# A guard's norms computed on TensorE instead of VectorE, and four lent buffers, in a planned attention kernel

## The chip, the cores and the metric

The kernel runs on one core of a Trainium2 chip. A core has engines with instruction streams of their own: TensorE (PE, with its weight loads PEld) multiplies matrices, VectorE (DVE) and ScalarE (ACT) work element by element, GpSimd (POOL) has little to do here, and SyncE (SP) issues transfers (DMAs). They tell each other of finished work by semaphores. Data lies in SBUF (128 partitions); TensorE's results arrive in PSUM, eight banks of 128 x 512 fp32. The metric is the time of one execution in microseconds (us), as the median of several runs.

## The reference

```python
def _A_ref(x, wqkv, wo):                      # x: 1 x 2048 x 640, 32 heads of 20
    qkv = (x @ wqkv).reshape(B, S, 3, H, Dh).transpose(2, 0, 3, 1, 4)
    q, k, v = qkv[0], qkv[1], qkv[2]
    scores = jnp.einsum("bhqd,bhkd->bhqk", q, k) * Dh ** -0.5
    p = softmax(scores)
    o = jnp.einsum("bhqk,bhkd->bhqd", p, v)
    return o.transpose(0, 2, 1, 3).reshape(B, S, D) @ wo

def _B_ref(x, w1, b1, w2):                    # 640 -> 1536 -> 640
    h = x @ w1 + b1
    sp = log1p(exp(-abs(h))) + where(h > 0, h, 0)
    return (h * tanh(sp)) @ w2                # mish

g = sigmoid((x * gate_w).sum(-1, keepdims=True))
out = g * _A_ref(x, wqkv, wo) + (1 - g) * _B_ref(x, w1, b1, w2)
```

Branch A is full attention, branch B a dense layer with the mish activation, and a gate per row mixes the two. All is bf16 with fp32 accumulation. The work that counts is the exponential: 32 heads x 2048 x 2048 scores.

## The kernel before, in words

**Units and slots.** The scores are computed in units of 128 keys x 512 queries of one head; there are 2048. Three units make a slot, 683 in all. For each slot TensorE writes the scores into three PSUM banks (`score_mms`, L1058), ScalarE turns all of them into bf16 exponentials by one instruction (`emit_e`, L1080, buffer `ETS`), and TensorE multiplies these with the values into one accumulating bank (`pv`, L1183), four heads side by side. Two sets of three banks take turns, so the scores of slot s + 2 may be written only when the exponentials of slot s have been read; meanwhile ScalarE works on slot s + 1. The last bank (`FB`) serves all other products.

**Units on VectorE.** In some slots the third unit isn't left to ScalarE, whose instruction is then two units wide (128 x 1024). VectorE computes its exponential in four instructions: `emit_x` reads the scores out of PSUM (L1097), two steps of a polynomial run in `EM` or `ER` (L1113), and a last one writes the result (L1115). The unit lives in a home: a buffer of 128 x 512 of four bytes. There are five (`UNITS`), used in turn: two in `XE` and three in a work area that lies in `W2R` and later in `REG`. A home is busy until the value product has read it. `choose` decides slot by slot whether a unit goes to VectorE, by VectorE's backlog and by when the unit's group ends (`CHAIN` is part of that sum). Before, 207 units go there.

**Groups.** 64 units of a group (one block of 512 queries, four heads) accumulate in one bank. VectorE copies it out (`OUNG`, L1261); three small transfers on SyncE's queue and VectorE's reciprocal and product (L1229) normalise it.

**Other tasks.** Between the slots TensorE does the rest in pieces of a few matmuls, as tasks with due slots: key, query and value projections (`kq_task` L539, `k_task` L591, `v_task` L685, `v_pair_task` L712), the first layer of branch B (`h_task`, L848, in half-chunks `hc` of 256 rows, with the bias added on VectorE, L858, into `HB`), its second layer (`b_task`, L909, whose output goes to `XS` for the first two row blocks and later to parts of `XB`), and the output projection (`p_task`, L933 and L939).

**The planner.** The kernel is built by a plan in Python: `Plan.add` puts an instruction on an engine's list and keeps an estimated clock per engine, from costs per instruction (`EXP`, `WIDE`, `PASS`). The loop over slots emits a slot's exponential, then the scores of the slot after next, value products and portions of due tasks, as far as the estimated time allows. VectorE's pieces wait in lists and are placed into estimated gaps (`work`). `fill_up` repeats scores or issues a spare product (L1442) where the estimated share of streaming columns of TensorE in a window falls below `STREAM` or `SPUN`. So the order on each engine is fixed when the kernel is built, and any change of a cost, a limit or a task moves all later instructions.

**The guard.** The softmax subtracts no maximum. A guard bounds the scores by the norms of the rows of queries' and keys' weights and of x: it computes the largest column sums of squares. Before, `squares` squares Wq, Wk and x on VectorE (40 instructions, L754) into `HB`, in eight tasks `sq_task`; TensorE sums each over the partitions with a column of ones (L770), and VectorE takes the maximum of the one row that results (L779). `flag_ops` combines the eight maxima (L1357 to L1363) into `FLAG`, which every engine loads (L1372); if it is set, a second program does everything again with maxima. It isn't set for these inputs. `h_task` waits until all eight squares have been read, since they lie in `HB`.

The functions that the change touches follow, with the line numbers of the profile.

Of the kernel before, what the change touches and what calls it, by code (L numbers as in the profile page):

```python
# [51 lines left out]
STREAM = 0.49  # L52
# [11 lines left out]
CHAIN = 3.3  # L64
# [32 lines left out]
UNITS = 5  # L97
ULPS = 128 / math.log(2)
# [118 lines left out]
def bass_gated_mix__softmax_full_mha__dense_activation_mish__prompt_kernel(  # L217
# [51 lines left out]
    MXS = sb("MXS", [1, 8], FP32)  # L269
    MXR = sb("MXR", [1, 4], FP32)  # L270
# [6 lines left out]
    def xt(c):  # L277
        return XB[:, c, :].rearrange("p (f t) -> p f t", t=CW)
# [29 lines left out]
    def ei(home):  # L308

        area, b = home  # L310
        return XE[:, b - 3, :] if b >= 3 else AREAS[area][1][:, b * CW:(b + 1) * CW]
# [22 lines left out]
    def attention(pl, fast):  # L334
# [122 lines left out]
        if fast:  # L457
# [284 lines left out]
            sq_ops, sq_read, sq_max = {}, {}, []  # L742

            def sq_src(n):
                return (WQ, WK)[n // 2][:, :, n % 2 * HALF:(n % 2 + 1) * HALF] if n < 4 else xt(n - 4)

            def squares(n):

                src = sq_src(n)
                after = [w_load[k] for k in (("wq", "wq0"), ("wk", "wk0"))[n // 2]] if n < 4 else xt_load[n - 4]  # L750

                def square(f):
                    dst = HB[:, n % 2, :, :].rearrange("p f t -> p (f t)")[:, f * CW:f * CW + src.shape[2]]
                    op = pl.add("dve", lambda e: e.tensor_tensor(dst, src[:, f, :], src[:, f, :], ALU.mult),  # L754
                                [*after, sq_read.get(n - 2)], cost=0.5)
                    sq_ops.setdefault(n, []).append(op)
                    if n < 4:
                        (wq_read, wkv_read)[n // 2].append(op)
                    else:
                        x_read[n - 4].append(op)  # L760

                for f in range(NFT):
                    bg.append((0.5, lambda f=f: square(f), lambda: max(after, key=lambda o: o.t1)))

            def sq_task(n, due):

                w = HALF if n < 4 else CW

                def mm(f):
                    return lambda e, bank: e.matmul(  # L770
                        PS[0:1, bank, 0:w], V_all[:, 0, 0, 0:1],
                        HB[:, n % 2, :, :].rearrange("p f t -> p (f t)")[:, f * CW:f * CW + w],
                        start=(f == 0), stop=(f == NFT - 1))

                def finish(bank, last):
                    sq_read[n] = last
                    if n + 2 < 8:
                        squares(n + 2)
                    ev = dve(lambda e: e.tensor_reduce(MXS[0:1, n:n + 1], PS[0:1, bank, 0:w], AX.X, ALU.max),  # L779
                             [last, *sq_max[-1:]], 0.69)  # L780
                    sq_max.append(ev)
                    if n == 7:
                        bg.append((0.5, lambda: flag_ops(ev), None))
                    return ev

                return Task([mm(f) for f in range(NFT)], w * COL, finish, due,
                            lambda: [*sq_ops[n], m_one] if len(sq_ops.get(n, ())) == NFT else None)
# [4 lines left out]
            def load_w1(n):  # L792

                k = n % 6
                if n < 2:
                    deps = []
                elif n in (FIRST, FIRST + 1):
                    assert len(sq_ops) >= 4
                    deps = list(wkv_read)
                else:  # L800
                    deps = [w1_last[n - 2]]
# [11 lines left out]
            def load_wo():  # L813
                assert len(sq_ops) >= 4
# [25 lines left out]
            def h_task(hc, k, due):  # L840
# [11 lines left out]
                def finish(bank, last):  # L852
                    x_read[c].append(last)
                    w1_last[n1] = last
                    if n1 + 2 < FIRST or FIRST <= n1 < 6 * NHC - 2:
# [4 lines left out]
                        [last, *b1f, *sq_read.values(), *b_read.get(hc - 2, [])], WIDE)  # L860
# [827 lines left out]
```

## Time and profile before

| | |
|---|---|
| median of 3 runs | 874.08 us (873.82 to 874.53) |
| the profiled execution | 874.34 us |
| its span, first to last instruction | 871.9 us |
| busy: ScalarE, VectorE, TensorE | 855.7, 831.2, 753.4 us |
| granted TensorE clock, mean | 0.998 |
| exponentials on ScalarE | 475 of three units, 208 of two |

Engine times are unions of the records. Records of ScalarE and TensorE overlap their neighbours, since an instruction is recorded from its entry into the engine's pipe to its end; a mean duration is longer than the pace at which instructions follow each other. In groups, the columns are the line, engine, operation, output and inputs with shapes, and the count; then busy time, the mean of one in ns, and the idle time ahead of it with what ended it. In the timeline the first two columns are the start and the length in us of a row, which may merge several instructions (xN).

### The profile page before, as it was taken

To read this page: it belongs to the slowest core of one execution; us is meant where nothing else is said; L and a number is where in the kernel's file an instruction comes from. 1 tells how busy PE (TensorE), PEld (TensorE's weight loads), DVE (VectorE), ACT (ScalarE), POOL (GpSimd) and SP (SyncE) were. 2 spreads that over 40 slices of the span, in tenths; PEclk is the share of its full clock that TensorE was granted. 3 is DMA by queue.
4 is the path that set the end of the run, shared out by engine and by line. 5 is a ranking of instruction groups with operands and counts; after the bars stand their busy time and mean duration, and the time that the engine had idled before them with its cause. 6 is when DMAs were issued, how large, how long until landed. Compare 5 with 4: busy or idle time off the path is not lost.

```text
span 871.9 us, 15314 instructions
## 1 busy us (share of the span) xinstructions
PE 753.4 (86%) x6244; PEld 258.2 (30%) x6293; DVE 831.2 (95%) x1441; ACT 855.7 (98%) x714; POOL 15.7 (2%) x29
## 2 busy tenths in 40 slices
PE   7888888889888888898888888898888888998895
PEld 3222332223322232232222333232333333332232
DVE  4899999999999999999999999999999999999995
ACT  6999999999999999999999999999999999999996
POOL 2000000000000000000000000000000000000000
PEclk9999999999999999999999999999999999999999
DMA  9112100012222111311111211111212112010001
GB/s 211 34 50 67 56 27 13 3 43 63 58 71 70 42 41 44 104 32 39 44 48 47 71 43 47 32 32 56 63 38 66 53 47 68 16 33 14 14 14 35
DMA packets 69870, 42.44 MB, mean 49 GB/s; under 512 B 20472, under 2 KB 65776, under 8 KB 69744
## 3 DMA queue, kind: packets, MB, share of 16 engines
q1 hardware_dynamic: 67424, 40.89, 16.5%
q8 instruction: 52, 0.85, 0.4%
q10 hardware_dynamic: 2256, 0.47, 0.3%
q0 software_dynamic: 112, 0.01, 0.2%
q14 instruction: 26, 0.21, 0.1%
HBM read 33.97 MB, written 5.23 MB: 45 GB/s over the span
## 4 chain that ended last, share of the span: by engine, by line
ACT 95%; PE 2%; DMA 1%; DVE 1%; SPq 0%; issue 0%; ACTq 0%
ACT ETS L1080 92%; ACT REG L880 2%; DMA BCT<-SUMS 1%; DMA OTN<-in_A_x_dram 1%; ACT W2R L880 1%; PE PS L1058 1%; PE PS L1183 0%; PE PS L539 0%; PE PS L909 0%; PE PS L659 0%; DVE HB L939 0%; DVE XE L1097 0%; PE PS L650 0%; SPq L583 0%; PE PS L1442 0%
## 5 line engine op out<-in xcount | busy, mean ns | idle before, releaser
L1080 ACT ACTIVATE ETS<-PS 128x1536 bf16<-128x1536 f32 (+1 forms) x683 | 836.6, 1501 | 0.8 <-PE PS L1058 0.7
L1058 PE MATMUL PS<-QT,KT 32*128 32x512 bf16 (+1 forms) x2191 | 275.9, 377 | 99.4 <-ACT ETS L1080 85.5
L1183 PE MATMUL PS<-ETS,V_all 128*21 128x512 bf16 (+1 forms) x1897 | 210.6, 379 | 1.0 <-ACT ETS L1080 0.5
L1058 PEld LDWEIGHTS PS<-QT,KT 32*128 32x128 bf16 x2191 | 68.3, 91 | 316.1 <-ACT ETS L1080 294.6
L1183 PEld LDWEIGHTS PS<-ETS,V_all 128*21 128x21 bf16 x1897 | 48.5, 89 | 95.9 <-issue 89.4
L909 PE MATMUL PS<-W2R,HB 128*128 128x320 bf16 x384 | 73.0, 302 | 0.4 <-DVE XB L916 0.2
L1113 DVE SCALAR_TENSOR_TENSOR EM<-EM 128x512 f32<-128x512 f32 x104 | 70.7, 679 | 0.1
L1113 DVE SCALAR_TENSOR_TENSOR ER<-ER 128x512 f32<-128x512 f32 x103 | 70.1, 681 | 0.0
L1097 DVE TENSOR_SCALAR XE<-PS 128x512 f32<-128x512 f32 x82 | 56.1, 684 | 3.2 <-PE PS L1058 1.9
L848 PE MATMUL PS<-XB,REG 128*128 128x256 bf16 x360 | 55.7, 275 | 1.2 <-DVE HB L858 0.6
L1097 DVE TENSOR_SCALAR REG<-PS 128x512 f32<-128x512 f32 x76 | 52.1, 686 | 4.0 <-PE PS L1058 2.6
L539 PE MATMUL PS<-XB,WOQ 128*128 128x512 bf16 x135 | 41.3, 383 | 2.8 <-issue 2.1
L909 PEld LDWEIGHTS PS<-W2R,HB 128*128 128x128 bf16 x384 | 28.7, 97 | 36.0 <-issue 23.3
L1097 DVE TENSOR_SCALAR W2R<-PS 128x512 f32<-128x512 f32 x49 | 33.4, 682 | 3.4 <-PE PS L1058 2.9
L848 PEld LDWEIGHTS PS<-XB,REG 128*128 128x128 bf16 x360 | 27.8, 97 | 26.8 <-issue 24.8
L858 DVE TENSOR_TENSOR HB<-PS,B1F 128x512 bf16<-128x512 f32 x48 | 32.7, 682 | 0.4 <-PE PS L848 0.3
L898 DVE SCALAR_TENSOR_TENSOR U<-U 128x512 f32<-128x512 f32 x48 | 32.7, 681 | 0.0
L899 DVE SCALAR_TENSOR_TENSOR U<-U,HB 128x512 f32<-128x512 f32 x48 | 32.5, 677 | 0.0
L1442 PE MATMUL PS<-KT 128*128 128x512 bf16 x100 | 30.2, 383 | 1.6 <-issue 1.3
L1113 DVE SCALAR_TENSOR_TENSOR EM<-XE 128x512 f32<-128x512 uint16 x41 | 28.0, 683 | 0.3
L1113 DVE SCALAR_TENSOR_TENSOR ER<-XE 128x512 f32<-128x512 uint16 x41 | 27.9, 681 | 0.2
L1115 DVE SCALAR_TENSOR_TENSOR XE<-ER,XE 128x512 int32<-128x512 f32 x41 | 27.9, 681 | 0.0
(115 smaller groups left out, 815.7 us busy)
## 6 DMA issues: line engine op xcount, KB each, us to landing
REG<-in_B_w_dram SPq DMA_DIRECT2D x36, 320.0 KB, 3.2
BCT<-SUMS SPq DMA_DIRECT2D x31, 256.0 KB
W2R<-in_B_w_dram SPq DMA_DIRECT2D x12, 320.0 KB, 3.3
KT<-KS SPq DMA_DIRECT2D x28, 128.0 KB
KS<-OTN SPq DMA_DIRECT2D x16, 128.0 KB, 1.7
W2R<-in_B_w_dram SPq DMA_DIRECT2D x1, 1920.0 KB, 7.9
out_dram<-OUTT SPq DMA_DIRECT2D x24, 80.0 KB, 1.6
REG<-in_A_wqkv_dram SPq DMA_DIRECT2D x2, 700.0 KB, 8.6
```

Source lines behind the costliest of these rows:

```text
L539: return lambda e, bank: e.matmul(PS[:, bank, :], pads[:, b, f, :], xt(c)[:, f, :], start=(f == 0), stop=(f == NFT - 1))
L848: return lambda e, bank: e.matmul(PS[:, bank, i * HW:(i + 1) * HW], w1b(n1)[:, f, i * P:(i + 1) * P], xt(c)[:, f, cols], start=(f == 0), s ...
L858: ev = dve(lambda e: e.tensor_tensor(hb, PS[:, bank, :].rearrange("p (i t) -> p i t", i=2), bias, ALU.add), [last, *b1f, *sq_read.values() ...
L898: piece(WIDE, lambda e: e.scalar_tensor_tensor(U2[:, :], U2[:, :], EVEN[0], U2[:, :], ALU.add, ALU.mult))
L899: piece(WIDE, lambda e, to=to: e.scalar_tensor_tensor(U2[:, :], U2[:, :], EVEN[1], to, ALU.add, ALU.mult))
L909: return lambda e, bank: e.matmul(PS[:, bank, 0:HALF], HB[:, hc % 2, f, t * P:(t + 1) * P], W2[:, f, half * HALF:(half + 1) * HALF], start ...
L1058: op = pl.add("pe", lambda e, i=i, g=real(g), tile=tile, j=j, cols=cols, c=c, of_q=of_q: e.matmul(scores(s)[:, i, cols], KT[32 * j:32 * j ...
L1080: e_op[s] = pl.add("act", lambda e: e.activation(ETS[:, s % NETS, 0:n, :], scores(s)[:, 0:n, :], AF.Exp, scale=SCALE, bias=LIFT if fast el ...
L1097: ev_op[s] = dve(lambda e: e.tensor_scalar(y, scores(s)[:, 2, :], SCALE * ULPS, BIAS, ALU.mult, ALU.add), [s_op[s], ei_free[b], *(wkv_read ...
L1113: piece(WIDE, lambda e, v=m if i else f, i=i: e.scalar_tensor_tensor(m, v, STEPS[i], v, ALU.add, ALU.mult), lambda i=i: () if i else [lane ...
L1183: lasts[n] = pl.add("pe", lambda e, tile=tile, h=real(g) * HG + j, j=j, src=src[:, cols], of_q=of_q, count=count: e.matmul(PS[32 * j:32 * ...
L1442: pl.add("pe", lambda e: e.matmul(PS[:, bank, :], k[:, 0:P], k, start=True, stop=True), [free], cost=PASS, kind="S")
```

## The change

Three things change together.

- The guard's column sums of squares are the diagonals of products of a block of 128 columns with itself. `gram_task` has TensorE multiply each block of Wq, Wk and x by itself, five row tiles accumulated: four blocks to a bank, seven tasks (130 products of 128 x 128). VectorE takes one maximum per bank over all entries (an entry off the diagonal can't exceed the largest on it). The result is a maximum per partition, so `flag_ops` first combines columns on 128 partitions, then a transfer on SyncE's queue puts 128 x 3 numbers into one row (`U2`), and `flag_end` takes their maximum and goes on as before.
- Since nothing is squared into `HB`, its second half (until half-chunk 1 writes it) and `XS` (until the first row blocks of branch B do) are lent as four more homes (`LENT`). `home` now takes the free home that has been free longest. `back` ends the lending, and the first writers wait for the value products that read them.
- `CHAIN` goes from 3.3 to 3.9 and `STREAM` from 0.49 to 0.48.

With these limits the plan puts 211 units on VectorE.

```diff
 EXP = 1.335
-STREAM = 0.49
+STREAM = 0.48
 SPUN = 0.6
...
 RISK = {"pe": 0.1, "act": 0.3, "dve": 0.5, "pool": 1.2, "sp": 0.6}
-CHAIN = 3.3
+CHAIN = 3.9
 AHEAD = 14
...
 UNITS = 5
+LENT = (("h", 0), ("h", 1), ("h", 2), ("x", 0))
 ULPS = 128 / math.log(2)
...
     GW = sb("GW", [P, NFT], BF16)
-    MXS = sb("MXS", [1, 8], FP32)
-    MXR = sb("MXR", [1, 4], FP32)
+    MXS = sb("MXS", [P, 8], FP32)
+    MXR = sb("MXR", [P, 4], FP32)
     FLAG = sb("FLAG", [1, 1], I32)
...
         area, b = home
+        if area == "h":
+            return HB[:, 1, 4 * b:4 * b + 4, :].rearrange("p f t -> p (f t)").bitcast(I32)
+        if area == "x":
+            return XS[:, 0:2 * CW].bitcast(I32)
         return XE[:, b - 3, :] if b >= 3 else AREAS[area][1][:, b * CW:(b + 1) * CW]
...
-            sq_ops, sq_read, sq_max = {}, {}, []
-
-            def sq_src(n):
-                return (WQ, WK)[n // 2][:, :, n % 2 * HALF:(n % 2 + 1) * HALF] if n < 4 else xt(n - 4)
-
-            def squares(n):
-
-                src = sq_src(n)
-                after = [w_load[k] for k in (("wq", "wq0"), ("wk", "wk0"))[n // 2]] if n < 4 else xt_load[n - 4]
-
-                def square(f):
-                    dst = HB[:, n % 2, :, :].rearrange("p f t -> p (f t)")[:, f * CW:f * CW + src.shape[2]]
-                    op = pl.add("dve", lambda e: e.tensor_tensor(dst, src[:, f, :], src[:, f, :], ALU.mult),
-                                [*after, sq_read.get(n - 2)], cost=0.5)
-                    sq_ops.setdefault(n, []).append(op)
-                    if n < 4:
-                        (wq_read, wkv_read)[n // 2].append(op)
+            grams = {}
+            guarded = []
+
+            def gram_task(n, due):
+
+                both = (w_load["wq"], w_load["wq0"], w_load["wk"], w_load["wk0"])
+                needs = both[0:2] if n == 0 else both[2:4] if n == 1 else both if n == 2 else xt_load[n - 3]
+                blocks = [(WQ, WK)[n] for _ in range(4)] if n < 2 else [WQ, WK] if n == 2 else [xt(n - 3)] * 4
+
+                def mm(b, f):
+                    at = 4 if n == 2 else b
+                    block = blocks[b][:, f, at * P:(at + 1) * P]
+                    return lambda e, bank: e.matmul(
+                        PS[:, bank, b * P:(b + 1) * P], block, block, start=(f == 0), stop=(f == NFT - 1))
+
+                def finish(bank, last):
+                    for reads in ([wq_read], [wkv_read], [wq_read, wkv_read])[n] if n < 3 else [x_read[n - 3]]:
+                        reads.append(last)
+                    if n == 2:
+                        to, src = MXS[:, 1:4:2], PS[:, bank, 0:2 * P].rearrange("p (a b) -> p a b", b=P)
                     else:
-                        x_read[n - 4].append(op)
-
-                for f in range(NFT):
-                    bg.append((0.5, lambda f=f: square(f), lambda: max(after, key=lambda o: o.t1)))
-
-            def sq_task(n, due):
-
-                w = HALF if n < 4 else CW
-
-                def mm(f):
-                    return lambda e, bank: e.matmul(
-                        PS[0:1, bank, 0:w], V_all[:, 0, 0, 0:1],
-                        HB[:, n % 2, :, :].rearrange("p f t -> p (f t)")[:, f * CW:f * CW + w],
-                        start=(f == 0), stop=(f == NFT - 1))
-
-                def finish(bank, last):
-                    sq_read[n] = last
-                    if n + 2 < 8:
-                        squares(n + 2)
-                    ev = dve(lambda e: e.tensor_reduce(MXS[0:1, n:n + 1], PS[0:1, bank, 0:w], AX.X, ALU.max),
-                             [last, *sq_max[-1:]], 0.69)
-                    sq_max.append(ev)
-                    if n == 7:
-                        bg.append((0.5, lambda: flag_ops(ev), None))
-                    return ev
-
-                return Task([mm(f) for f in range(NFT)], w * COL, finish, due,
-                            lambda: [*sq_ops[n], m_one] if len(sq_ops.get(n, ())) == NFT else None)
+                        to, src = MXS[:, (0, 2, 0, 4, 5, 6, 7)[n]:][:, 0:1], PS[:, bank, :]
+                    grams[n] = dve(lambda e: e.tensor_reduce(to, src, AX.X, ALU.max), [last], WIDE)
+                    if len(grams) == 7:
+                        bg.append((0.3, lambda: flag_ops(grams.values()), None))
+                    return grams[n]
+
+                return Task([mm(b, f) for b in range(len(blocks)) for f in range(NFT)], 0.06, finish, due,
+                            lambda: list(needs))
...
                 elif n in (FIRST, FIRST + 1):
-                    assert len(sq_ops) >= 4
+                    assert all(n in grams for n in range(3))
                     deps = list(wkv_read)
...
             def load_wo():
-                assert len(sq_ops) >= 4
+                assert all(n in grams for n in range(3))
                 wo_v = A_wo.rearrange("(g j r) c -> j r g c", g=NG, j=HG, r=DH)
...
                         hb, PS[:, bank, :].rearrange("p (i t) -> p i t", i=2), bias, ALU.add),
-                        [last, *b1f, *sq_read.values(), *b_read.get(hc - 2, [])], WIDE)
+                        [last, *b1f, *guarded, *b_read.get(hc - 2, []), *lent("h", hc == 1)], WIDE)
                     if k % 2:
...
                 def ready():
-                    if len(acts) > 1 or len(sq_read) < 8 or n1 not in w1_load or (hc >= 2 and len(b_read.get(hc - 2, ())) < 4):
+                    if len(acts) > 1 or not guarded or n1 not in w1_load or (hc >= 2 and len(b_read.get(hc - 2, ())) < 4):
+                        return None
+                    if hc == 1 and not back("h"):
                         return None
...
                         OMG[:, tb:tb + 1], None, ALU.mult),
-                        [last, gate_done[0], *(x_read[(hc - 1) // 2] if hc else ())], HALVED)
+                        [last, gate_done[0], *(x_read[(hc - 1) // 2] if hc else lent("x"))], HALVED)
                     bdone[(tb, half)] = ev
...
                         return None
-                    if any((hc, k) not in h_done for k in range(6)):
+                    if any((hc, k) not in h_done for k in range(6)) or hc == 0 and not back("x"):
                         return None
...
         ei_free.update({(None, b): None for b in range(3, UNITS)})
+        ei_free.update({at: None for at in LENT})
+        given_back = set()
         area = [0]
...
+        def lent(name, here=True):
+
+            return [op for at, op in ei_free.items() if here and at[0] == name and op is not None]
+
+        def back(name):
+
+            given_back.add(name)
+            return "busy" not in lent(name)
+
         def home():
-            b = nx[0] % UNITS
-            return (None if b >= 3 else area[0], b)
+            some = [(None if b >= 3 else area[0], b) for b in range(UNITS)]
+            some += [at for at in LENT if at[0] not in given_back]
+            some = [at for at in some if ei_free[at] != "busy"]
+            return min(some, key=lambda at: ei_free[at].t1 if ei_free[at] else 0.0, default=None)
...
             ev_op[s] = dve(lambda e: e.tensor_scalar(y, scores(s)[:, 2, :], SCALE * ULPS, BIAS, ALU.mult, ALU.add), [
-                s_op[s], ei_free[b], *(wkv_read if b[0] else ())], WIDE)
+                s_op[s], ei_free[b], *(wkv_read if b[0] == 1 else ())], WIDE)
             last = [ev_op[s]]
...
             urgent, other = (sum(t[0] for todo in some for t in todo) for some in ((norm, *soon), (blend, bg)))
-            if (len(order) < SLOT or ei_free[home()] == "busy"
+            if (len(order) < SLOT or home() is None
                     or late + urgent + other >= BEHIND):
...
             assert all(t.due < last_kv.due for t in tasks[tasks.index(last_q) + 1:-1])
-            tasks.extend(sq_task(n, SQ + SQ_STEP * n) for n in range(8))
+            tasks.extend(gram_task(n, SQ + SQ_STEP * n) for n in range(7))
             tasks.extend(h_task(hc, k, H_AT + int(H_STEP * (6 * hc + k))) for hc in range(2) for k in range(6))
...
-        def flag_ops(last):
-
-
-            m = MXR[0:1, :]
+        def flag_ops(deps):
+
+            m = MXR[:, :]
+            row = U2[0:1, 0:3 * P]
             a = pl.add("dve", lambda e: e.tensor_reduce(
-                m, MXS[0:1, :].rearrange("o (a b) -> o a b", b=2), AX.X, ALU.max), [last])
+                m, MXS[:, :].rearrange("p (a b) -> p a b", b=2), AX.X, ALU.max), list(deps))
             a = pl.add("dve", lambda e: e.tensor_tensor(m[:, 2:3], m[:, 2:3], m[:, 3:4], ALU.max), [a])
+            moved = pl.add("sp", lambda e: e.dma_start(row, m[:, 0:3], allow_slow_non_contiguous=True), [a], "mx", tail=4.0)
+            bg.append((0.8, lambda: flag_end(row, moved), lambda: moved))
+
+        def flag_end(row, moved):
+
+            m = MXR[0:1, 0:3]
+            a = pl.add("dve", lambda e: e.tensor_reduce(
+                m, row.rearrange("o (p a) -> o a p", a=3), AX.X, ALU.max), [moved], cost=0.5)
+            guarded.append(a)
             for n in (2, 0, 1):
...
                 load_w2()
-            if fast and step == SQ - 18:
-                squares(0)
-                squares(1)
             if acts and safe(acts[0][0]) < pl.now["act"] and mish_free():
```

## The prediction

> **What bounds the kernel now.** I read the page first, then ScalarE's instructions by form, the chain that ended last in order of time, and the busy time of the engines (PE, its weight loads, DVE, ACT, POOL, then the clock) in the stretch of the exponentials and after it.
>
> ```profile
> span 871.9 us, 15314 instructions
> PE 753.4 (86%) x6244; PEld 258.2 (30%) x6293; DVE 831.2 (95%) x1441; ACT 855.7 (98%) x714; POOL 15.7 (2%) x29
> PEclk9999999999999999999999999999999999999999
> ACT 95%; PE 2%; DMA 1%; DVE 1%; SPq 0%; issue 0%; ACTq 0%
> ```
>
> ```profile
> L1080 ACT ACTIVATE ETS<-PS 128x1536 bf16<-128x1536 f32 x475 | 679.1, 1626 | 0.8 <-PE PS L1058 0.7
> L1080 ACT ACTIVATE ETS<-PS 128x1024 bf16<-128x1024 f32 x208 | 233.2, 1215 | 0.0
> ```
>
> ```profile
> 635.55 0.94 ACT REG L880
> 636.49 15.76 ACT ETS L1080 x13
> 652.24 0.94 ACT REG L880
> 653.18 16.18 ACT ETS L1080 x13
> ```
>
> ```profile
> 10.50:863.05 852.55, 742.63 (x6182) 253.44 (x6228) 823.08 (x1425) 852.23 (x708) 10.48 (x19) 1.00 0.16 47
> 863.05:871.90 8.85, 2.68 (x18) 1.21 (x19) 2.99 (x7) 0.53 (x1) 0.86 (x1) 0.83 0.19 56
> ```
>
> The exponentials on ScalarE are the kernel: 683 slots, 475 of them three units wide and 208 two wide (207 slots whose third unit is computed on VectorE, and the last slot, which has only two). From 10.50 to 863.05 us ScalarE is busy for 852.23 of 852.55 us, with them and 24 tanh at 0.94 us. The records overlap, so their means are no pace. The stretches of 13 exponentials are: 16.18 and 15.76 us differ by 0.42, one two-wide slot more. The pace itself, and what is lost to waits too short to show as idle, is in the timeline:
>
> ```profile
> 77.07 4.82 ACT L1080 ACTIVATE ETS<-PS 128x1536 bf16<-128x1536 f32 x4
> 78.76 0.39 PE L1058 MATMUL PS<-QT,KT 32*128 32x512 bf16 x3 [0.40 <-ACT ETS L1080]
> 79.08 0.40 PE L1183 MATMUL PS<-ETS,V_all 128*21 128x512 bf16 x4
> 79.64 0.38 PE L539 MATMUL PS<-XB,WOQ 128*128 128x512 bf16 x1 [0.16 <-DVE EM L1113]
> 79.95 0.39 PE L1058 MATMUL PS<-QT,KT 32*128 32x512 bf16 x3
> ```
>
> ```profile
> 78.40 1.22 ACT L1080 ACTIVATE ETS<-PS 128x1024 bf16<-128x1024 f32 x1
> 79.30 1.24 ACT L1080 ACTIVATE ETS<-PS 128x1024 bf16<-128x1024 f32 x1
> 80.39 1.50 ACT L1080 ACTIVATE ETS<-PS 128x1536 bf16<-128x1536 f32 x1
> ```
>
> A three-wide slot starts at 77.07 and the next at 78.40: 1.33 us. A two-wide one takes 0.90 (78.40 to 79.30). But the second two-wide in a row lasts 1.09, to 80.39: its successor's scores started only at 79.95, 1.19 after the scores before them (78.76), because TensorE had four value products and projections to do between. So 0.19 us is lost with no idle time on the page. A worse one shows as idle:
>
> ```profile
> 272.12 0.39 PE L1058 MATMUL PS<-QT,KT 32*128 32x512 bf16 x3
> 272.45 0.82 PE L539 MATMUL PS<-XB,WOQ 128*128 128x512 bf16 x3
> 273.20 0.40 PE L1183 MATMUL PS<-ETS,V_all 128*21 128x512 bf16 x4
> 273.53 0.69 PE L1058 MATMUL PS<-QT,KT 32*128 32x512 bf16 x6
> 273.96 1.45 ACT L1080 ACTIVATE ETS<-PS 128x1536 bf16<-128x1536 f32 x1 [0.20 <-PE PS L1058]
> ```
>
> Three projections and four value products lay between scores 1.41 us apart, 0.5 more than ScalarE's 0.90; of that 0.20 shows as idle time. At 1.33 and 0.90 the exponentials come to 475 x 1.33 + 208 x 0.90 = 819; 852.6 less the tanh (24 x 0.94 = 22.6) is 830. So 10 to 11 us are lost to such lateness (9.7 when I add it up start by start). Sorted by what the program orders between two scores, 6.8 of it falls on slots that follow two two-wide slots. So the bound is ScalarE, and behind two two-wide slots it is TensorE.
>
> **The change part by part.** *Units.* The order of the changed kernel has 212 two-wide slots instead of 208 and 471 three-wide. Saved on ScalarE: 4 x 0.43 = 1.7 us, all of it on the chain. By the two forms' means it is 4 x 0.41 (1626 less 1215 ns), by the stretches 4 x 0.42: 1.6 to 1.7.
>
> *Where they lie.* The planner moves everything, so lateness is counted anew in TensorE's order. I weigh the matmuls between two scores at these spacings: 0.22 us for a projection of 512 columns (0.82 less 0.38, over two), 0.14 for 320, 0.11 for 256, 0.06 for 128, 0.22 for a group of value products. Before, slots behind two two-wide ones:
>
> - over 0.7 us of work: 10 of them, 2.8 us lost (0.28 each; first at 38.91 us, last the one below);
> - 0.6 to 0.7: 19, 2.8 us lost (0.15 each; that of 80.39 is one);
> - less: 42, 1.1 us lost.
>
> ```profile
> 843.68 1.34 ACT L1080 ACTIVATE ETS<-PS 128x1024 bf16<-128x1024 f32 x1
> 844.98 1.02 ACT L1080 ACTIVATE ETS<-PS 128x1024 bf16<-128x1024 f32 x1
> ```
>
> Here 1.30 us passed instead of 0.90. In the changed order there are 18 of the first kind, 12 of the second and 34 of the third; three of the 18 (slots 9, 73, 141) have the very three projections and four value products of 273.96. At the same prices: 18 x 0.28 + 12 x 0.15 + 0.9 = 7.7, so 0.9 more than 6.8. The other slots lost 2.9; slots behind one two-wide slot with over 0.8 us of work grow from 21 to 37, at 0.04 each, so 0.6 more. Taken: 1.5 us more lateness. The ends: at 0.19 for each of the 18, 0.05 of the 12 and 0.9 it is 4.9, 1.9 less than now; at 0.40 and 0.25 it is 11.1, 4.3 more. I take the means, since they are from the same patterns, and keep the ends for the range.
>
> *VectorE.*
>
> ```profile
> L754 DVE TENSOR_TENSOR HB<-XB 128x512 bf16<-128x512 bf16 x20 | 8.1, 415 | 0.0
> L754 DVE TENSOR_TENSOR HB<-REG 128x320 bf16<-128x320 bf16 x10 | 3.1, 315 | 1.1 <-PE PS L770 1.1
> L754 DVE TENSOR_TENSOR HB<-WOQ 128x320 bf16<-128x320 bf16 x10 | 3.1, 340 | 0.0
> L779 DVE TENSOR_REDUCE MXS<-PS 1x1 f32<-1x512 f32 x4 | 2.7, 672 | 0.0
> L779 DVE TENSOR_REDUCE MXS<-PS 1x1 f32<-1x320 f32 x4 | 1.9, 476 | 0.3 <-PE PS L770 0.3
> L1097 DVE TENSOR_SCALAR XE<-PS 128x512 f32<-128x512 f32 x82 | 56.1, 684 | 3.2 <-PE PS L1058 1.9
> ```
>
> Removed: 8.1 + 3.1 + 3.1 + 2.7 + 1.9 = 18.9 us. Added: six maxima over 128x512 at 0.67 (the row is of one partition; the 128-partition read of PSUM in the last row is 0.68), a seventh over half as much at 0.4, one over 384 elements at 0.5, and four units of four instructions at 0.68 = 10.9; together 15.8. VectorE is 3 us lighter of 831. On the path: nothing, it released no late score in the cases I followed.
>
> *TensorE.*
>
> ```profile
> L770 PE MATMUL PS<-HB,V_all x40: 297/338/379, 33.7 to 206.5; 128*1 128x320 bf16 x20, 128*1 128x512 bf16 x20
> 6.39 1.01 PEld L650 LDWEIGHTS PS<-OTN 128*128 128x128 bf16 x18 [0.91 <-DMA OTN<-in_A_x_dram]
> 6.39 1.18 PE L650 MATMUL PS<-OTN 128*128 128x128 bf16 x18 [0.73 <-DMA OTN<-in_A_x_dram]
> ```
>
> Forty products leave, at 0.14 and 0.22: 7.2 us. The 130 of 128x128, each with its own weights, come: at 1.18/18 = 0.066 they are 8.5 us, in 16 portions of 3 to 13 between scores. Their load lies beside the matmul in that row; this is already in the counting above. The Trainium skill ("TensorE: Matmul & The Clock Gate", Back-to-back issue gap) gives about 81 ns for such a pair in a stream. By it the 130 would take 10.5 us, 2 more, and the sum would be at most 875.9; the trace's 66 ns is the measurement, and I keep it.
>
> *The guard's end.* One transfer and one more maximum come ahead of the flag.
>
> ```profile
> SUMS<-RR SPq DMA_DIRECT2D x31, 8.0 KB, 1.4
> GW<-in_gate_w_dram POOLq DMA_DIRECT2D x1, 1.2 KB, 6.1
> ```
>
> 128 rows go through SyncE's queue: 1.4 us by the nearest row (128 rows of 64 bytes), 6.1 by the worst small one. The planner issues the reader 4 us later. At 6.1 VectorE would stand 2.1 us with queued reads of scores behind it: between 0 and 2.1, I take 0. On SyncE the transfer waits for the maximum, and the next group's sums queue behind it. The planner puts it where that maximum is done, and a group lasts some 20 slots: 0. The lent homes cost the same instruction as other homes. What is late if they come back late is the bias addition of the second half-chunk and the first scaled output; both follow in order long after the value products that free them: 0.
>
> *Start and end.* The start up to 10.50 and the last 60 instructions of VectorE are in the same order: 0.
>
> Sum, against the profiled run (874.34 us; span 871.9 and 2.4 around it; 0.26 over the median of 874.08): -1.7 + 1.5 = -0.2. **873.9 us** by the median.
>
> **The rivals.** *The whole gain arrives*: lateness stays at 9.7 because a pair costs by chance what its neighbours allow (some pairs of over 0.6 us of work lost nothing). -1.7 plus 4 x 0.04 (9.7 over 208) = -1.5: 872.5; with lateness like the cheap end, 870.5. For it: prices scatter from 0 to 0.5. Against: twice as many crowded pairs.
>
> *Slower, by weights that are not hidden*: the 130 products load weights and stream from one tile, and if load and matmul took turns, each would cost 0.056 more (1.01/18). A portion of eight lengthens by 0.45 us; where no slack takes it up that is 16 x 0.45 = 7.2 more, 881. It decides from 0.12 us a portion on. Against: the 18 loads above lay inside 1.18 us.
>
> *Slower, by the clock*: the re-issue of scores that keeps TensorE streaming asks for a share of 0.48 instead of 0.49, and 10 score matmuls fewer are issued.
>
> ```profile
> 1.20 4.35 PE L491 MATMUL PS<-ETS 128*128 128x512 bf16 x10 [1.20 <-DVE ETS L478]
> ```
>
> At the start a matmul of 512 takes 0.43 us, twice the 0.22 of later; and at the end, where TensorE is busy for 2.68 of 8.85 us, the granted clock falls to 0.83. A slot at half speed needs 1.2 us more; two such dips give 876.3. Against: PEclk is full in all 40 slices, through thinner stretches than this change makes. The Trainium skill (the same page, "A second HAM failure mode") says that micro-idling between groups of matmuls can swing the clock to half; no stretch of this trace before its end does that.
>
> **How the numbers follow.** The measurement tells 0.2%, 1.75 us, from nothing: 872.3 to 875.8. My forecast 0.58, the gain whole 0.27 (a good half of it beyond 872.3), weights 0.05, clock 0.04, a late transfer or home 0.06. Of the forecast's own spread (one to one and a half us) a tenth lies beyond either bound. Faster 0.21, same 0.64, slower 0.15. Range 871.6 to 876.0, the likeliest one's own 872.4 to 875.4.
>
> **What would show it.** Two-wide slots 212; their pace 0.90 and 1.33 unchanged; the new products some 0.06 us apart; 0.4 to 0.5 us lost around slots 9, 73 and 141; VectorE 3 us less busy. I am wrong if lateness over the whole chain does not grow, or grows by more than 3 us, if the granted clock dips inside the chain, or if ScalarE waits at the flag.

## The result and the profile after

The changed kernel takes 872.64 us (median of 13 runs, 871.74 to 873.27) and the kernel before, timed beside it, 874.0 us (13 runs, 873.3 to 875.52): a ratio of 0.9982, with a 95% interval of 0.9973 to 0.999. It is faster by 0.18%, a gain that the interval tells from nothing and that lies within the 0.2% up to which the prediction calls two times the same. The forecast of 873.9 was 1.3 us too high; the rival in which the whole gain arrives (872.5) is 0.1 off.

The page of the changed kernel, and its exponentials among ScalarE's instructions by form:

```profile
span 870.5 us, 15507 instructions
PE 764.5 (88%) x6377; PEld 263.2 (30%) x6377; DVE 830.9 (95%) x1417; ACT 854.7 (98%) x714; POOL 16.3 (2%) x29
PEclk9999999999999999999999999999999999999999
ACT 97%; PE 2%; DVE 0%; issue 0%; ACTq 0%
```

```profile
L1072 ACT ACTIVATE ETS<-PS 128x1536 bf16<-128x1536 f32 x471 | 673.8, 1609 | 0.7 <-PE PS L1050 0.5
L1072 ACT ACTIVATE ETS<-PS 128x1024 bf16<-128x1024 f32 x212 | 238.1, 1195 | 0.3 <-PE PS L1050 0.3
```

Two-wide slots are 212 instead of 208, ScalarE is as full as before, the granted clock is full in all slices. The stretch of the exponentials, from the first start to the last end (columns: the stretch, PE, PEld, DVE, ACT, POOL, clock, DMA share, GB/s):

```profile
9.87:861.59 851.72, 753.45 (x6314) 258.47 (x6312) 822.81 (x1401) 851.19 (x708) 11.06 (x19) 1.00 0.17 47
861.59:870.49 8.90, 2.83 (x19) 1.22 (x19) 2.99 (x7) 0.53 (x2) 0.86 (x1) 0.93 0.21 58
```

It lasts 851.72 us, 0.83 less than the 852.55 of before. The stretch after it is 8.90 (8.85 before), and the first exponential starts at 9.87 (10.50 before). So of the 1.4 us between the two spans 0.8 lies in the stretch, 0.6 in the start and nothing at the end.

I added up lateness start by start as in the prediction: the time from one exponential's start to the next, less 1.33 or 0.90 (1.330 and 0.904 to a further digit) and less what ScalarE does between. It was 9.7 us before and is 10.6 now. The three slots with the very pattern of 273.96 show it in ScalarE's timeline; the first, then the second and third:

```profile
19.71 1.07 ACT L1072 ACTIVATE ETS<-PS 128x1024 bf16<-128x1024 f32 x1
21.12 1.02 ACT L1072 ACTIVATE ETS<-PS 128x1024 bf16<-128x1024 f32 x1 [0.34 <-PE PS L1050]
...
96.25 1.34 ACT L1072 ACTIVATE ETS<-PS 128x1024 bf16<-128x1024 f32 x1
97.65 1.45 ACT L1072 ACTIVATE ETS<-PS 128x1536 bf16<-128x1536 f32 x1
...
177.09 1.34 ACT L1072 ACTIVATE ETS<-PS 128x1024 bf16<-128x1024 f32 x1
178.50 1.45 ACT L1072 ACTIVATE ETS<-PS 128x1536 bf16<-128x1536 f32 x1
```

From 19.71 to 21.12 is 1.41 for a two-wide slot worth 0.90, from 96.25 to 97.65 is 1.40, from 177.09 to 178.50 is 1.41: 0.50 lost in each, as at 273.96 before.

### The profile page after: what moved, and what is told of

Its sections match the earlier page's. It is cut to its first block, busy times and chain, and to the rows that moved or that the text cites. A ratio compares the mean times of both kernels' runs of the same rounds, so it can differ in the third digit from the quotient of the medians.

```text
span 870.5 us, 15507 instructions
## 1 busy us (share of the span) xinstructions
PE 764.5 (88%) x6377; PEld 263.2 (30%) x6377; DVE 830.9 (95%) x1417; ACT 854.7 (98%) x714; POOL 16.3 (2%) x29
## 4 chain that ended last, share of the span: by engine, by line
ACT 97%; PE 2%; DVE 0%; issue 0%; ACTq 0%
ACT ETS L1072 94%; ACT REG L870 2%; ACT W2R L870 1%; PE PS L496 1%; PE PS L1050 0%; PE PS L1186 0%; PE PS L596 0%; PE PS L544 0%; PE PS L664 0%; DVE HB L929 0%; PE PS L655 0%; PE PS L1454 0%; PE PS L923 0%; PE PS L643 0%; ACT KT L639 0%
## 5 line engine op out<-in xcount | busy, mean ns | idle before, releaser
L1186 PE MATMUL PS<-ETS,V_all 128*21 128x512 bf16 (+1 forms) x1893 | 207.4, 379 | 0.9 <-ACT ETS L1072 0.5
L1116 DVE SCALAR_TENSOR_TENSOR EM<-EM 128x512 f32<-128x512 f32 x106 | 72.5, 684 | 0.1
L1116 DVE SCALAR_TENSOR_TENSOR ER<-ER 128x512 f32<-128x512 f32 x105 | 71.9, 685 | 0.1
L1100 DVE TENSOR_SCALAR XE<-PS 128x512 f32<-128x512 f32 x71 | 48.7, 687 | 6.4 <-PE PS L1050 5.4
L544 PE MATMUL PS<-XB,WOQ 128*128 128x512 bf16 x155 | 46.3, 384 | 0.0
L1454 PE MATMUL PS<-KT 128*128 128x512 bf16 x119 | 35.4, 384 | 0.0
L1116 DVE SCALAR_TENSOR_TENSOR EM<-REG 128x512 f32<-128x512 uint16 x38 | 26.1, 688 | 0.2
L1118 DVE SCALAR_TENSOR_TENSOR REG<-EM,REG 128x512 int32<-128x512 f32 x38 | 26.1, 687 | 0.1
L1116 DVE SCALAR_TENSOR_TENSOR ER<-REG 128x512 f32<-128x512 uint16 x37 | 25.4, 688 | 0.1
L1118 DVE SCALAR_TENSOR_TENSOR REG<-ER,REG 128x512 int32<-128x512 f32 x37 | 25.4, 687 | 0.1
```

What stands on the lines that cost most here:

```text
L544: return lambda e, bank: e.matmul(PS[:, bank, :], pads[:, b, f, :], xt(c)[:, f, :], start=(f == 0), stop=(f == NFT - 1))
L1100: ev_op[s] = dve(lambda e: e.tensor_scalar(y, scores(s)[:, 2, :], SCALE * ULPS, BIAS, ALU.mult, ALU.add), [s_op[s], ei_free[b], *(wkv_read ...
L1116: piece(WIDE, lambda e, v=m if i else f, i=i: e.scalar_tensor_tensor(m, v, STEPS[i], v, ALU.add, ALU.mult), lambda i=i: () if i else [lane ...
L1118: piece(WIDE, lambda e: e.scalar_tensor_tensor(x, m, LAST_STEP, y, ALU.mult, ALU.add))
L1186: lasts[n] = pl.add("pe", lambda e, tile=tile, h=real(g) * HG + j, j=j, src=src[:, cols], of_q=of_q, count=count: e.matmul(PS[32 * j:32 * ...
L1454: pl.add("pe", lambda e: e.matmul(PS[:, bank, :], k[:, 0:P], k, start=True, stop=True), [free], cost=PASS, kind="S")
```

## The experiments

Each kernel is timed against the kernel before on the same chip. Edits are to the changed kernel unless said.

### The two kernels again

No edit. The theory was that the profiled start (10.50 us before) belongs to the execution and not to the kernel.

> The kernel before, unchanged, for a second profile. Theory (the start is not the change's): its first exponential starts anywhere between 9.8 and 10.6 us, as the first load of x lands, and from there to the end of the last exponential it takes 852.5 us again, within 0.3, with 9.7 us of lateness. Rival (the change moved the start): the first exponential is at 10.5 again, within 0.1.

> The changed kernel, unchanged, for a second profile and more timed runs. Theory: the stretch of the exponentials is 0.8 us shorter than before (851.7), since four units save 1.7 and lateness has grown by 0.9 (10.6), and the rest of the difference of the medians is the landing of the first load; 500 ns are lost again at slots 9, 73 and 141. Rival (the change moved the start): first exponential at 9.87 again, within 0.1.

Measured: before 873.79 (22 runs; the one profiled 873.85), changed 872.91 (11 runs, 871.78 to 873.92), ratio 0.999 (0.9981 to 0.9999). The stretches, first of the kernel before, then of the changed kernel:

```profile
9.75:863.18 853.43, 752.16 (x6230) 253.41 (x6228) 823.33 (x1425) 852.45 (x708) 10.59 (x19) 1.00 0.17 47
```

```profile
10.30:862.03 851.73, 753.41 (x6314) 258.45 (x6312) 822.81 (x1401) 851.19 (x708) 10.88 (x19) 1.00 0.16 47
```

The changed kernel repeats its stretch to 0.01 us. Its start now is the later one (10.30 against 9.75): over all my profiles the first exponential lies between 9.75 and 10.56 us, whatever the kernel. The start is not the change's: so far the theory held.

But the kernel before doesn't repeat, and here the theory missed: 853.43 against 852.55, where a repeat within 0.3 was expected. Slot by slot its lateness is the same, except at two slots 4 us apart (263.27 and 267.33) that lost 0.48 and 0.39 more; it is 10.6 in all. Its VectorE and TensorE there:

```profile
259.71 0.68 DVE L1113 SCALAR_TENSOR_TENSOR EM<-EM 128x512 f32<-128x512 f32 x1
261.96 0.69 DVE L1229 TENSOR_TENSOR OTN<-OUNG,BCT 128x512 bf16<-128x512 f32 x1 [1.57 <-DMA BCT<-SUMS]
262.57 0.68 DVE L901 SCALAR_TENSOR_TENSOR HB<-W2R,U 128x512 bf16<-128x512 f32 x1
263.17 0.68 DVE L599 CAST OTN<-PS 128x512 bf16<-128x512 f32 x1
```

```profile
264.00 0.71 PE L848 MATMUL PS<-XB,W2R 128*128 128x256 bf16 x5 [0.59 <-DVE OTN L599]
264.64 0.39 PE L1058 MATMUL PS<-QT,KT 32*128 32x512 bf16 x3
```

VectorE waits 1.57 us for the broadcast of a group's sums, a bank of keys is copied out late behind it, TensorE waits 0.59 for that bank, and the scores follow late. In the first profile this wait was 0.7, and ScalarE lost almost nothing by it (0.04). The groups of VectorE's product by those sums, in the second profile of before and in the first of the changed kernel (the last column is idle time ahead of it):

```profile
L1229 DVE TENSOR_TENSOR OTN<-OUNG,BCT 128x512 bf16<-128x512 f32 x16 | 10.9, 683 | 1.6 <-DMA BCT<-SUMS 1.6
```

```profile
L1232 DVE TENSOR_TENSOR OTN<-OUNG,BCT 128x512 bf16<-128x512 f32 x16 | 11.0, 685 | 0.0
```

The changed order has no such wait in either profile. So lateness is 9.7 or 10.6 before, by one transfer's landing, and 10.6 after.

### No more units than before

```diff
-            if (len(order) < SLOT or home() is None
+            if (len(order) < SLOT or home() is None or nx[0] >= 207
```

> The changed kernel with one condition more: no unit goes to VectorE after the 207th, so the last four stay on ScalarE, and all before them is as in the changed kernel. Theory (the gain is the four units, less lateness): 208 two-wide slots, the stretch of the exponentials 1.4 to 1.7 us longer than the changed kernel's, 874.0 us. Rival (the gain comes from the lighter VectorE, or from elsewhere in the guard): it stays at 872.6.

Measured: 873.95 us (11 runs, 872.92 to 875.93), ratio 1.0005 (0.9996 to 1.0014): as long as before, and 1.04 longer than the changed kernel on the same chip. Its stretch:

```profile
10.32:863.69 853.37, 755.12 (x6321) 258.75 (x6319) 813.33 (x1385) 852.83 (x708) 11.12 (x19) 1.00 0.16 47
```

The two orders are the same up to the slots where the last four units are dropped. Lateness is 10.17, 0.43 less, since a crowded slot goes with the units. From the first start to the last start it is 1.3 us longer (851.82 against 850.56), which is 4 x 0.43 less that 0.43; to the last end it is 1.65 longer (853.37 against 851.72, expected 1.4 to 1.7), since the record of the last exponential is longer too, 1.54 against 1.17. So without the four units the change is worth nothing that the interval tells, and the rival is out. VectorE's busy time falls by 9.5 us for the 16 instructions, 0.59 each.

### The new guard without homes and constants

```diff
-STREAM = 0.48
+STREAM = 0.49
-CHAIN = 3.9
+CHAIN = 3.3
-LENT = (("h", 0), ("h", 1), ("h", 2), ("x", 0))
+LENT = ()
```

> The products on TensorE alone: the changed kernel without the four lent homes, and with CHAIN 3.3 and STREAM 0.49 as before. Its order has 214 two-wide slots (213 units on VectorE), two more than with the whole change. Slots behind two two-wide ones: 21 with over 0.7 us of other work on TensorE, 19 with 0.6 to 0.7. Theory (four units per 1.7 us, less lateness by the counted slots): 0.85 us less on ScalarE than the changed kernel, 1.1 more lateness: 873.1 us. Rival (the lent homes make the gain): like the kernel before, 873.8 or more.

Measured: 872.84 us (11 runs, 872.19 to 873.61), ratio 0.9987 (0.9978 to 0.9996), where the expectation was 873.1. There are 214 two-wide slots, two more than with lent homes, and lateness is 11.8: two units gain 0.86 and 1.2 more is late. So the units come without the lent homes and the new constants. This kernel keeps one more thing of the change, the rule by which `home` picks a free home; no run takes that rule away by itself, so how much of the six units more is the guard's and how much the rule's isn't shown.

### Lent homes taken away alone, and the constants alone

The first edit:

```diff
-LENT = (("h", 0), ("h", 1), ("h", 2), ("x", 0))
+LENT = ()
```

> The changed kernel without the four lent homes, CHAIN and STREAM as changed. 212 two-wide slots as in the changed kernel, but 26 crowded slots of over 0.7 us and 15 of 0.6 to 0.7, instead of 18 and 12. Theory: 2.1 us more lateness, 874.9 us. Rival (units alone decide): 872.8 us.

The second, to the kernel before:

```diff
-STREAM = 0.49
+STREAM = 0.48
-CHAIN = 3.3
+CHAIN = 3.9
```

> The kernel before with CHAIN 3.9 and STREAM 0.48 alone. 208 two-wide slots as before, but 20 crowded slots of over 0.7 us instead of 10, and 9 instead of 19 of 0.6 to 0.7. Theory: 1.5 us more lateness than before, 875.3 us. Rival (units alone decide): 873.8 us.

The constants alone take 875.33 us (10 runs, 873.93 to 877.24), ratio 1.0014 (1.0004 to 1.0024): the number that was expected, but in part by luck. Slots behind two two-wide ones lost 7.2 us, only 0.5 more than before, while a dip of TensorE's granted clock cost another 0.95 at 284.9 to 288.5 us (its windows are in the last section). Without lent homes and with the new constants it is 877.18 (5 runs, 876.15 to 880.59), ratio 1.0047 (1.003 to 1.0064), 2.3 more than expected: 212 two-wide slots, but 14.0 us of lateness. Three slots of it, 2.9 us, are large. One is this, on VectorE and ScalarE (the third column is the engine):

```profile
96.77 0.25 DVE L1271 RECIPROCAL RR<-RR 128x16 f32<-128x16 f32 x1 [1.44 <-DMA RR<-OUNG]
...
99.66 3.71 ACT L1072 ACTIVATE ETS<-PS 128x1024 bf16<-128x1024 f32 x3 [1.14 <-PE PS L1050]
```

and VectorE's waits for that transfer over the whole run (us, times, longest):

```profile
DVE RR L1271 <- DMA RR<-OUNG: 3.1, 2, 1.6
```

So with `CHAIN` at 3.9 and `STREAM` at 0.48 the homes do matter, though not by units: the order that results without them runs into two late transfers of a group's sums. The slots behind these lost 1.43 and 0.80, 2.2 of the 3.4 us of lateness that this order has over the changed kernel's. That a home as such costs or gains time isn't shown.

### No two two-wide slots in a row

In the prediction 6.8 of 9.7 us were lost behind two two-wide slots. If the second slot of a pair is the cause, an order without pairs has nearly none of that; if TensorE's work is late wherever it is put, lateness moves to other slots.

```diff
-            if (len(order) < SLOT or home() is None
+            if (len(order) < SLOT or home() is None or s - 1 in off
```

> The changed kernel with one condition more: a slot gives no unit to VectorE if the slot before it did. The order has 211 two-wide slots and no two in a row. Theory (TensorE is late for slots behind two two-wide ones): their 6.7 us of lateness go, the single ones take some 1 us more, 0.4 us more on ScalarE; total lateness 4.7 instead of 10.6, some 866.9 us. Rival (TensorE's whole load is the limit, so it is late elsewhere instead): lateness stays near 10 and the time at 872 to 873.

Measured: 876.16 us (6 runs, 874.96 to 877.9), ratio 1.0031 (1.0018 to 1.0043). There are 211 two-wide slots, none behind another, and 13.3 us of lateness. Two slots lost 1.55 and 1.52, waiting for value products:

```profile
303.65 1.45 ACT L1072 ACTIVATE ETS<-PS 128x1536 bf16<-128x1536 f32 x1 [1.38 <-PE PS L1186]
306.49 1.45 ACT L1072 ACTIVATE ETS<-PS 128x1536 bf16<-128x1536 f32 x1 [1.40 <-PE PS L1186]
```

two lost 1.36 while the clock was at half, in the second of these windows:

```profile
494.90:498.30 3.40, 2.38 (x24) 0.81 (x23) 3.40 (x6) 3.40 (x4) 0.00 (x0) 1.00 0.25 72
498.30:501.70 3.40, 3.40 (x18) 0.99 (x14) 2.55 (x5) 2.81 (x3) 0.00 (x0) 0.50 0.30 103
```

and the rest is spread over slots behind a single two-wide one. Four more kernels try to give the same rule an order without these mishaps: more repeated scores against the clock, a longer landing time in the plan for the transfer that comes late below (`tail`), the old `CHAIN`.

```diff
+STREAM = 0.53                                  # nopair_s53
+..., "nr0", cost=0.55, tail=1.8)               # nopair_s53_t18, beside 0.53 (was 1.4)
+STREAM = 0.59; CHAIN = 3.3                     # nopair_s59_c33
+STREAM = 0.56; CHAIN = 3.3                     # nopair_s56_c33
```

> No two two-wide slots in a row, as in the kernel nopair, and STREAM 0.53 instead of 0.48, so that more scores are repeated to keep TensorE streaming. 211 two-wide slots. In nopair the granted clock fell to half twice, for 3.4 us at 498 and at 860 us, and cost 1.4 and some 1.0 us there; 3.1 us went at 303 to 306 us, where ScalarE waited for value products. Theory (TensorE too thin for its clock is what ate the gain): no dip, 2.4 us less than nopair from that, and 866 to 870 us, by whether the wait for value products is there again. Rival (TensorE's whole load is the limit): lateness of 10 or more again, 872 us or more.

> As nopair_s53 (no two two-wide slots in a row, STREAM 0.53), but the planner takes 1.8 instead of 1.4 us for the landing of a group's sums, so that VectorE's reciprocal is ordered later. 210 two-wide slots. In nopair_s53 that reciprocal stood 2.4 us at 96.7 us, the scores behind it came late, TensorE ran thin and its clock fell to half for 6.8 us: 3.75 us between slots 73 and 78. Theory (the late transfer is what ate the gain there): no such wait, clock full, lateness of 5 to 8 us, 868 to 870 us. Rival (TensorE has no room for it): lateness of 10 or more again, 872 us or more.

> No two two-wide slots in a row, STREAM 0.59 and CHAIN 3.3, the landing as before. 211 two-wide slots. Theory: the clock stays full through the exponentials; if no reciprocal waits for its transfer, lateness of 5 to 8 us, 868 to 870 us; if one does, 1 to 3 us more. Rival (repeated scores now fill TensorE and make it late itself): 872 us or more at a full clock.

> No two two-wide slots in a row, STREAM 0.56 and CHAIN 3.3. 211 two-wide slots. Theory: as for STREAM 0.59, 867 to 870 us where neither the clock falls nor a reciprocal waits for its transfer. Rival: 872 us or more at a full clock.

| kernel | median us (range, runs) | ratio to before (95%) | lateness of the profiled run, us |
|---|---|---|---|
| `STREAM` 0.53 | 872.5 (871.38 to 874.54, 11) | 0.9981 (0.9972 to 0.999) | 12.1 |
| and `tail` 1.8 | 872.43 (871.87 to 873.66, 11) | 0.9986 (0.9977 to 0.9995) | 9.0 |
| `STREAM` 0.59, `CHAIN` 3.3 | 872.27 (871.39 to 874.32, 11) | 0.9983 (0.9974 to 0.9992) | 9.9 |
| `STREAM` 0.56, `CHAIN` 3.3 | 872.14 (871.45 to 873.66, 11) | 0.9981 (0.9972 to 0.999) | 9.9 |

All four missed: I expected 866 to 870, and their ratios lie within the intervals of the changed kernel's. Each has its own late transfer at the same place. Of the first, VectorE, TensorE and ScalarE:

```profile
96.67 0.25 DVE L1271 RECIPROCAL RR<-RR 128x16 f32<-128x16 f32 x1 [2.41 <-DMA RR<-OUNG]
97.39 0.68 DVE L1100 TENSOR_SCALAR HB<-PS 128x512 f32<-128x512 f32 x1
...
98.21 0.39 PE L1050 MATMUL PS<-QT,KT 32*128 32x512 bf16 x3 [1.46 <-DVE HB L1100]
...
98.65 2.36 ACT L1072 ACTIVATE ETS<-PS 128x1536 bf16<-128x1536 f32 x2 [0.93 <-PE PS L1050]
```

The reciprocal waits 2.41 us, the read of scores queued behind it is late, TensorE can't overwrite that bank for 1.46, and ScalarE stands 0.93. With `tail` at 1.8 the wait is 1.3, with the other two 2.0 and 2.2. Even taking this place and the clock away, some 8 us of lateness stay, with no pair at all: lone two-wide slots and the three-wide ones behind them now lose 8.5 to 11 us, where such slots lost 2.7 before. The four also repeat more scores, which is more work for TensorE (2215 to 2418 score matmuls, against 2186 in the first order without pairs). But that first order keeps 7.5 us once its dips and its waits are taken away, and the four keep 8.2 to 8.4 however many scores they repeat, so the repeats are not what fills the gap. This speaks for the rival: most lateness goes with what TensorE has to do beside the exponentials, and pairs mostly decide where it is paid. No run lightens TensorE's work alone, so it isn't shown outright.

## Why the prediction was right, and where it wasn't

*Units*, -1.7: right. 212 two-wide slots at unchanged paces; the order without the four units takes 1.3 us more from first to last start and 1.04 by the medians, since a crowded slot goes with them.

*Where they lie*, +1.5: too much. This term made about half of the 1.3 us by which the forecast was high. By the same sorting of slots:

| slots | predicted | measured |
|---|---|---|
| behind two two-wide, over 0.7 us of work | 18 x 0.28 = 5.0 | 4.86 |
| 0.6 to 0.7 | 12 x 0.15 = 1.8 | 1.29 |
| less | 0.9 | 0.55 |
| behind one two-wide, over 0.8 | 37 x 0.04 = 1.5 | 1.30 |
| the others | 2.1, as before | 2.58 |

The crowded class was priced within 4%, and slots 9, 73 and 141 lost 0.500, 0.498 and 0.500, the top of the 0.4 to 0.5 that was said. The two lighter classes lost 0.9 less than priced: their prices were means over cases that differ widely, and the new order drew cheaper ones. The others lost 0.5 more than taken. So lateness grew by 0.9 instead of 1.5 against the profile that I worked from.

The other half of the error is that profile. Its lateness of 9.7 holds one landing that happened to be harmless; in the second profile the same wait cost 0.9, and against that one lateness didn't grow at all: -1.7 (853.43 to 851.73) is just the units. Between -0.8 and -1.7 lies the measured -1.4 (-0.9 in the other batch). How often that landing is late in the timed runs can't be seen, and no run took it away, so how the 0.9 is shared between the change and chance stays open. The test that I set, lateness that doesn't grow, is met by one profile of before and not by the other.

*VectorE*, 3 us lighter, nothing on the path: nothing on the path is right, 3 us is not. Its busy time in the stretch fell by 0.3 (823.08 to 822.81). I took records' lengths (0.68), but they overlap as ScalarE's do: instructions follow each other 0.60 apart (262.57 and 263.17 above). Four units cost 9.5 by the run without them, not 10.9, and what the guard takes off is 9.8 (823.08 to 813.33), not 14.0 (18.9 less the maxima's 4.9). The maxima came as priced, but for the last, 0.7 instead of 0.5:

```profile
L769 DVE TENSOR_REDUCE MXS<-PS 128x1 f32<-128x512 f32 x6 | 4.1, 685 | 0.0
L1369 DVE TENSOR_REDUCE MXR<-U 1x3 f32<-1x384 f32 x1 | 0.7, 655 | 0.0
```

*TensorE*, 8.5 for 7.2: near, and it cost nothing that shows. The new products between two scores:

```profile
48.69 0.68 PE L759 MATMUL PS<-REG 128*128 128x128 bf16 x9
49.39 0.39 PE L1050 MATMUL PS<-QT,KT 32*128 32x512 bf16 x3
49.71 0.79 PE L759 MATMUL PS<-REG 128*128 128x128 bf16 x11
```

Two more products take 0.11 us more: 0.055 each, 0.066 predicted. Weights load beside them, so the rival at 881 is out. The Trainium skill ("TensorE: Matmul & The Clock Gate", Back-to-back issue gap) has 81 ns for such pairs in a stream; the trace, in portions of 9 and 11 pairs, doesn't agree, and its 55 decides. TensorE's busy time in the stretch rose by 1.3 (752.16 in the complete record of before to 753.45), as much as the sum had, but by luck: at 0.055 the 130 come to 7.2, no more than the forty that left, and other matmuls changed in number too.

*The guard's end*, 0: right. The transfer took 2.0 us, between the two bounds, and ScalarE didn't wait at the flag:

```profile
U<-MXR SPq DMA_DIRECT2D x1, 1.5 KB, 2.0
```

*The clock rival* didn't happen here, but its price was right in size: dips that cost 1.4 and about 0.95 us appear in two experiments; a third, with `STREAM` at 0.53, has a longer one (6.8 us) that can't be told from its late transfer. *Late transfer or home*: not in the changed kernel, but two late transfers are a good part of why the order without lent homes is 4.5 us slower than the changed one.

## What to carry to other kernels

Where an order is written out in advance, count what an edit gains at pace (here 0.43 us a unit) and price what it shifts from slots of the same pattern: the heavy pattern repeated within 4% in the changed kernel, the light ones didn't. This goes for orders that are much alike: with the constants alone and the new guard alone the heavy pattern cost 0.23 and 0.29 a slot against the 0.28 priced, and the forecast for the order without pairs, priced by the same classes, was 9 us too low, some 5 of them from dips and waits that no class held. Profile the kernel before twice: one transfer that lands late or not moved its stretch by 0.9 us, as much as the whole change. And take the pace of an engine from start to start, since records that overlap make every removed instruction look dearer than it is.

## What the hardware did that I had not expected

**The granted clock falls with TensorE more than half busy.** In the order with the constants alone, ahead of a dip and in it, and in the kernel before (second profile) at a thin place without a dip:

```profile
280.80:284.20 3.40, 1.96 (x17) 0.42 (x14) 3.34 (x7) 3.40 (x4) 0.00 (x0) 1.00 0.13 44
284.20:287.60 3.40, 3.40 (x21) 0.78 (x19) 3.40 (x6) 3.25 (x3) 0.00 (x0) 0.50 0.09 34
```

```profile
314.70:318.10 3.40, 2.12 (x27) 1.02 (x27) 3.40 (x6) 3.40 (x4) 0.00 (x0) 1.00 0.33 113
```

TensorE was busy for 1.96 of 3.40 us ahead of the dip, and for 2.12 at the place without one; so a dip doesn't need an idle window. Busy time alone isn't the measure either: the dip in the order without pairs came after 2.38, and another window of that order with 1.95 (303.74 to 307.15) was followed by none. What sets a dip off stays open. The Trainium skill ("TensorE: Matmul & The Clock Gate", What's actually happening) puts the half clock behind an idle window of about 3.4 us; the length of the dip and its one level, half, agree with it, the idle window doesn't. Times follow these dips: of the runs without pairs, the one with a mean clock of 0.999 took 874.96 us, and the five at 0.991 to 0.995 took 875.84 to 877.9.

**Lateness is a property of the order.** Between two runs of one kernel it repeats within 0.01 us slot by slot, but for the one late transfer of the kernel before. The 8 KB transfers of a group's sums, in contrast, come 1.3 to 2.4 us late for VectorE in six different orders at nearly the same place, 95.5 to 96.8 us in.

**The late transfers share a place in SyncE's queue.** They are issued directly behind two transfers that lay out keys (`KT<-KS`, 128 KB each). SyncE's transfers around 92 us, first in the order without pairs at `STREAM` 0.53, where VectorE waited 2.41, then in the changed kernel, where it didn't wait:

```profile
90.83 1.10 SPq L588 DMA_DIRECT2D KT<-KS  x2
91.97 0.55 SPq L1267 DMA_DIRECT2D RR<-OUNG  x1
```

```profile
92.22 0.56 SPq L1267 DMA_DIRECT2D RR<-OUNG  x1
92.83 1.07 SPq L588 DMA_DIRECT2D KT<-KS  x2
```

Over all thirteen profiles VectorE stood for 7 of the 403 transfers `RR<-OUNG`: exactly the seven that were issued so. The four broadcasts `BCT<-SUMS` that it waited for, those of the kernel before among them, stand behind such a pair as well, but eight others that do made nobody wait. No run moves these transfers apart, so that the queue's order is the cause is likely, not shown.
